# Other places in the step order for the leftover blocks' stages and expert weights

## The chip, the cores and the metric

One core of one Trainium2 chip runs the whole program. The metric is device time in microseconds (us), as the median of three executions; the profile is of one further execution.

## What is computed

Agent attention, and then a mixture of experts that sends each token to one expert. B = 4, N = 11456 tokens, C = 128, 49 agents, 8 experts of 128 → 1024 → 128:

```python
def sm(a, b):
    s = scale * (a @ b.transpose(0, 2, 1))
    s = s - s.max(-1, keepdims=True)
    e = np.exp(s)
    return e / (e.sum(-1, keepdims=True) + 1e-09)
agent_v = sm(agents, k) @ v
x = (sm(q, agents) @ agent_v).reshape(B * N, C)
logits = x @ w_gate
expert_idx = np.argmax(logits, axis=1)
gate_w = softmax(logits)[np.arange(B * N), expert_idx]
for e in range(8):                       # out starts as zeros
    mask = expert_idx == e
    h = np.maximum(x[mask] @ w1[e], 0.0)
    out[mask] = gate_w[mask, None] * (h @ w2[e])
```

## The kernel before

**Main work.** For each batch one main expert is run densely on all tokens (`experts`), in 23 groups of four tiles of 128 tokens (the last of two of 96) times 8 slices of the hidden layer: 184 steps. A step is two matmuls into `ph` (L1198, L1199), a relu on ScalarE (L1204), the low half of the f16 pair `hh` on VectorE (L1205), and five steps later twelve matmuls into `py` (L1218). Two buffers of `ph` lie between TensorE and the other two, so a step's L1198 waits for an earlier step's L1205. Every eighth step a group is stored (L1231, and a DMA on SP, L1294). While a batch is in its experts, the attention of the next, or here of the batch's own last chunks, goes between the steps: transposes through SP (`hT` L387 and L391, `M` L630), matmuls on them (L415, L639), and the routing's small VectorE work.

**Leftover blocks.** Tokens whose expert isn't the batch's main one are run in blocks of 128. Twelve blocks, of batches 0 to 2, are prepared during the experts of the last batch in three groups of four (the first, second and third group here); two more, of all batches, make the late group. `prepare_blocks` prepares a group in stages:

- slot flags `fo` (L961), then rank indices `fri` (L971) and an indirect gather of `fg` on the POOL queue, one for each block (L222);
- the `fr` chain on VectorE (L983 to L1005), which reads `fg`, yields token indices `ftr` (L997), and gathers `fx` with them (L222);
- a ScalarE copy of `fx` (L1011), TensorE transposes of it (L1017), the copy `fae` (L1018), and small loads on SP (L1016);
- two matmul stages (L1023, L1032) that end in the block's scaled input `xs` (L1040, L1041).

Ahead of the second and the third of these stands a `hold`: the next relu of the main work takes a column of the hold's tile as its bias (then it stands as L1202), and the stage behind it needs that tile's buffer. So the stage can't be ordered ahead of that step, but earlier steps can run late and it may still wait for the gather.

**Weights.** `weights_ahead(u)` requests the two f32 matrices of block u's expert on SP (`w1e` L241, `w2e` L243). `weights_split(u, j)` makes an f16 pair of one of them, on ScalarE (L1057) and VectorE (L1059). Seven blocks' weights are requested and split in the last batch, the other seven in the loop behind it, where all blocks are computed.

**What sets the order.** Everything is pushed on a heap with a time in steps and emitted in the order of these times; the order is also the priority for the scheduler that fixes each engine's order of instructions, and it may bring ready work forward. The last batch begins at `l0`. A group begins at `l0 + FG + FGI * g`, its stages at the offsets of `FST` from there (`FLS` for the late group at `l0 + FL + 2`). Weights are requested at `l0 + FW + FWJ * u` and split `FS` steps later. SP, VectorE, ScalarE and TensorE each run their instructions in order, so one that waits holds those behind it. Steps are counted below from the first L1198 of the last batch.

Of the kernel before, what the change touches and what calls it, by code (L numbers as in the profile page):

```python
# [60 lines left out]


NSE, NSL, UG = 12, 2, 4
FE, FG, FGI, FST = 34, 38, 32, (0, 4, 11, 12.5, 21, 22.5, 30, 35)
FL, FLS, FW, FWJ, WA, FS, SPA, FSE = 152, (0, 2, 9, 10.5, 18, 19.5, 26, 29), 104, 10.5, 7, 8, 7, 'D'
TSE, BL = 'D', 2
AHEAD = 3

# [1298 lines left out]
```

## Time and profile before

| | |
|---|---|
| median of three executions | 1198.95 us (1197.06 to 1199.13) |
| profiled execution | 1206.96 us |
| its span, first to last instruction | 1205.3 us |
| mean granted TensorE clock | 0.943 of full speed |
| TensorE busy | 1046.4 us, 87% |
| VectorE busy | 1050.3 us, 87% |
| ScalarE busy | 853.1 us, 71% |

The profiled execution is 8.0 us longer than the median. Busy shares are means over the whole span; the experts of the last batch, in which all changed work lies, are the stretch from about 895 to 1146 us.

### The profile page before, as it was taken

To read this page: it belongs to the slowest core of one execution; us is meant where nothing else is said; L and a number is where in the kernel's file an instruction comes from. 1 tells how busy PE (TensorE), PEld (TensorE's weight loads), DVE (VectorE), ACT (ScalarE), POOL (GpSimd) and SP (SyncE) were. 2 spreads that over 40 slices of the span, in tenths; PEclk is the share of its full clock that TensorE was granted. 3 is DMA by queue.
4 is the path that set the end of the run, shared out by engine and by line. 5 is a ranking of instruction groups with operands and counts; after the bars stand their busy time and mean duration, and the time that the engine had idled before them with its cause. 6 is when DMAs were issued, how large, how long until landed. Compare 5 with 4: busy or idle time off the path is not lost. (4 is left out here: it accounts for less than half of the span.)

```text
span 1205.3 us, 36167 instructions
## 1 busy us (share of the span) xinstructions
PE 1046.4 (87%) x14654; PEld 839.7 (70%) x14654; DVE 1050.3 (87%) x2733; ACT 853.1 (71%) x1530; POOL 179.2 (15%) x234
## 2 busy tenths in 40 slices
PE   6666899988898899998987899999989898989895
PEld 5563677766777677777766677777767676767685
DVE  7768899989788899999978899999899888989685
ACT  8737788769658688779667797787575555756481
POOL 0120000015300000123300000225100112110123
PEclk9656999989898999999999999999999999999998
DMA  8449999552279799662399799450564545423370
GB/s 319 127 99 257 258 207 218 159 158 75 52 213 251 164 206 217 190 150 89 81 245 253 156 230 209 131 145 31 141 171 115 120 98 105 141 67 109 120 249 15
DMA packets 265675, 191.05 MB, mean 159 GB/s; under 512 B 217513, under 2 KB 230306, under 8 KB 265504
## 3 DMA queue, kind: packets, MB, share of 16 engines
q1 hardware_dynamic: 263936, 186.44, 61.0%
q0 software_dynamic: 1568, 2.25, 1.0%
q8 instruction: 116, 1.90, 0.6%
q14 instruction: 55, 0.45, 0.1%
HBM read 99.75 MB, written 36.43 MB: 113 GB/s over the span
## 5 line engine op out<-in xcount | busy, mean ns | idle before, releaser
L1218 PEld LDWEIGHTS <-hh 128*128 128x128 f16 x8640 | 557.1, 100 | 171.2 <-issue 12.8
L1218 PE MATMUL py<-w2h,hh 128*128 128x128 f16 (+1 forms) x5760 | 617.2, 222 | 3.4 <-issue 1.7
L1204 ACT ACTIVATE hh<-ph 128x512 f16<-128x512 f32 (+1 forms) x728 | 410.3, 584 | 195.6 <-PE ph L1199 181.7
L1218 PE MATMUL py<-w2l,hh 128*128 128x128 f16 (+1 forms) x2880 | 532.8, 222 | 0.5 <-issue 0.5
L1205 DVE SCALAR_TENSOR_TENSOR hh<-ph,hh 128x512 f16<-128x512 f32 (+1 forms) x736 | 479.2, 667 | 37.4 <-ACT hh L1204 33.6
L1198 PE MATMUL ph<-M,Ah 128*128 128x512 f16 (+1 forms) x736 | 280.1, 381 | 36.4 <-DVE hh L1205 30.3
L1199 PE MATMUL ph<-M,Al 128*128 128x512 f16 (+1 forms) x736 | 280.0, 381 | 0.0
L362 DVE SCALAR_TENSOR_TENSOR hl<-ld,mul,hl 128x1024 f16<-128x1024 f32 (+1 forms) x126 | 155.7, 1239 | 11.6 <-ACT hl L360 10.8
L360 ACT ACTIVATE hl<-ld,mul 128x1024 f16<-128x1024 f32 (+1 forms) x126 | 136.1, 1089 | 30.6 <-DVE mul L214 30.3
L328 ACT ACTIVATE jk<-ld 128x1024 f16<-128x1024 f32 (+1 forms) x138 | 139.0, 1007 | 25.7 <-DMA ld<-in_q_dram 18.8
L1199 PEld LDWEIGHTS <-Al 128*128 128x128 f16 x736 | 72.8, 99 | 41.4 <-issue 39.4
L415 PEld LDWEIGHTS <-hT 128*128 128x128 f16 (+1 forms) x630 | 53.4, 99 | 36.3 <-DMA hT<-hl 35.2
L624 POOL TENSOR_TENSOR mm<-E,mm 128x392 f16<-128x392 f32 (+1 forms) x18 | 19.8, 1103 | 393.6 <-DVE mm L620 348.7
L1198 PEld LDWEIGHTS <-Ah 128*128 128x128 f16 x736 | 74.1, 101 | 5.2 <-issue 2.5
L415 PE MATMUL ps_s<-agh,hT 128*128 128x49 f16 x572 | 54.5, 187 | 22.6 <-DMA hT<-hl 20.5
L1231 DVE TENSOR_TENSOR yo<-py,cs 128x512 f32<-128x512 f32 (+1 forms) x92 | 61.4, 667 | 0.3 <-PE py L1218 0.3
L416 PE MATMUL ps_s<-agl,hT 128*128 128x49 f16 x572 | 54.0, 186 | 0.6 <-issue 0.6
L417 PE MATMUL ps_s<-agh,hT 128*128 128x49 f16 x572 | 53.9, 186 | 0.5 <-issue 0.5
L416 PEld LDWEIGHTS <-hT 128*128 128x128 f16 (+1 forms) x630 | 52.7, 99 | 1.8 <-issue 1.4
L493 POOL TENSOR_TENSOR es<-es,S 128x392 f32<-128x392 f32 (+1 forms) x39 | 38.5, 988 | 99.2 <-ACT S L483 75.6
L417 PEld LDWEIGHTS <-hT 128*128 128x128 f16 (+1 forms) x630 | 52.7, 99 | 0.6 <-issue 0.3
L613 ACT ACTIVATE E<-E,ln,div 128x392 f32<-128x392 f32 (+1 forms) x48 | 33.2, 691 | 20.1 <-DVE E L608 20.0
(307 smaller groups left out, 1530.7 us busy)
## 6 DMA issues: line engine op xcount, KB each, us to landing
ld<-in_k_dram SPq DMA_DIRECT2D x44, 512.0 KB
ld<-in_v_dram SPq DMA_DIRECT2D x44, 512.0 KB
ld<-in_q_dram SPq DMA_DIRECT2D x44, 512.0 KB
out_dram<-yo SPq DMA_DIRECT2D x88, 256.0 KB
w1e<-in_moe_w_dram SPq DMA_DIRECT2D x18, 512.0 KB
w2e<-in_moe_w_dram SPq DMA_DIRECT2D x18, 512.0 KB
exps<-E SPq DMA_DIRECT2D x44, 196.0 KB
wn<-in_moe_w_dram SPq DMA_DIRECT2D x16, 512.0 KB
```

What stands on the lines that cost most here:

```text
L328: nc.scalar.activation(jk[:p, :t * D], x[:p, :t, :].rearrange("p t d -> p (t d)"), AF.Square, accum_out=ss[:p])
L360: nc.scalar.activation(hi[:p, :t, :], x[:p, :t, :], AF.Copy, scale=m)
L362: nc.vector.scalar_tensor_tensor(lo[:p, :t, :], x[:p, :t, :], m, hi[:p, :t, :], op0=ALU.mult, op1=ALU.subtract)
L415: nc.tensor.matmul(o, x[:, 0, i, :p], AG["h"], start=True, stop=False)
L416: nc.tensor.matmul(o, x[:, 0, i, :p], AG["l"], start=False, stop=False)
L417: nc.tensor.matmul(o, x[:, 1, i, :p], AG["h"], start=False, stop=True)
L1198: nc.tensor.matmul(ph[:, :nn], st['Ah'][:, f, :], m, start=True, stop=False)
L1199: nc.tensor.matmul(ph[:, :nn], st['Al'][:, f, :], m, start=False, stop=True)
L1204: nc.scalar.activation(hh[:, 0, :nn], ph[:, :nn], AF.Relu)
L1205: nc.vector.scalar_tensor_tensor(hh[:, 1, :nn], ph[:, :nn], 0.0, hh[:, 0, :nn], op0=ALU.max, op1=ALU.subtract)
L1218: mm_ = lambda l, r, **k: nc.tensor.matmul(o, l, r, skip_group_check=True, **k)
L1231: nc.vector.tensor_tensor(yo[:p, :n, :], py[:p, :n * D].rearrange("p (i d) -> p i d", d=D), cs.unsqueeze(2).broadcast_to([p, n, D]), op=AL ...
```

## The change

Only times in the step order change. The first group's table is built 4 steps earlier, the three groups begin at steps 34, 62 and 90 instead of 38, 70 and 102. The `fr` chain is planned 13.5 steps behind the request of its gather instead of 8.5, and the copy of `fx` 16 steps behind the `fr` chain instead of 10; the later stages move along. In the late group the distances become 11.5 and 12 instead of 8.5 and 9. Weights are requested from step 92 on instead of 104, and split 14 steps later instead of 8, so the first split is planned at 106 instead of 112.

```diff
 NSE, NSL, UG = 12, 2, 4
-FE, FG, FGI, FST = 34, 38, 32, (0, 4, 11, 12.5, 21, 22.5, 30, 35)
-FL, FLS, FW, FWJ, WA, FS, SPA, FSE = 152, (0, 2, 9, 10.5, 18, 19.5, 26, 29), 104, 10.5, 7, 8, 7, 'D'
+FE, FG, FGI, FST = 30, 34, 28, (0, 4, 16, 17.5, 32, 33.5, 40, 45)
+FL, FLS, FW, FWJ, WA, FS, SPA, FSE = 152, (0, 2, 12, 13.5, 24, 25.5, 30, 33), 92, 10.5, 7, 14, 7, 'D'
```

On VectorE, the late group's index chain L983, which reads the gather `fg`, and the steps' L1205 ahead of it. Before:

```order
L1205 SCALAR_TENSOR_TENSOR hh<-ph,hh 128x512
L1059 SCALAR_TENSOR_TENSOR wsp<-w1e,tsm_18812,wsp 128x1024
L1205 SCALAR_TENSOR_TENSOR hh<-ph,hh 128x512 x2
L1059 SCALAR_TENSOR_TENSOR wsp<-w2e,tsm_18816,wsp 128x1024
L1205 SCALAR_TENSOR_TENSOR hh<-ph,hh 128x512 x2
L983 TENSOR_TENSOR fr_22368<-tsl,fg 128x2
L1205 SCALAR_TENSOR_TENSOR hh<-ph,hh 128x512
L984 TENSOR_TENSOR fm<-fg,fr_22368 128x180
```

Now, from the index L971 that the gather is requested with:

```order
L971 TENSOR_TENSOR fri<-frf,trb 128x2
L1205 SCALAR_TENSOR_TENSOR hh<-ph,hh 128x512
L993 TENSOR_SCALAR fr_22448<-fpc 128x2
L1059 SCALAR_TENSOR_TENSOR wsp<-w1e,tsm_18738,wsp 128x1024
L1205 SCALAR_TENSOR_TENSOR hh<-ph,hh 128x512 x3
L1059 SCALAR_TENSOR_TENSOR wsp<-w2e,tsm_18742,wsp 128x1024
L1205 SCALAR_TENSOR_TENSOR hh<-ph,hh 128x512 x2
L1059 SCALAR_TENSOR_TENSOR wsp<-w1e,tsm_18738,wsp 128x1024
L1205 SCALAR_TENSOR_TENSOR hh<-ph,hh 128x512 x3
L1231 TENSOR_TENSOR yo<-py,cs 128x512
L1205 SCALAR_TENSOR_TENSOR hh<-ph,hh 128x512
L1059 SCALAR_TENSOR_TENSOR wsp<-w2e,tsm_18742,wsp 128x1024
```

Behind the last of these rows follow one L1205 and then L983. From L971 to L983 there are now eleven steps; before there were seven.

On TensorE, the late group's transposes L1017, which read the ScalarE copy of `fx`. Before:

```order
L1198 LDWEIGHTS Ah
L1198 MATMUL ph<-M,Ah 128x512
L1199 LDWEIGHTS Al
L1199 MATMUL ph<-M,Al 128x512
L1017 MATMUL ps_small<-ident,fx_22590 49x128 x2
L1218 LDWEIGHTS hh
L1218 MATMUL py<-w2h,hh 128x128
```

Now, where ScalarE makes the copy behind the relu of step 179:

```order
L1218 LDWEIGHTS hh
L1218 MATMUL py<-w2h,hh 128x128
L1017 MATMUL ps_small<-ident,fx_22705 49x128 x2
L1198 LDWEIGHTS Ah
L1198 MATMUL ph<-M,Ah 128x192
L1199 LDWEIGHTS Al
L1199 MATMUL ph<-M,Al 128x192
```

L1017 went from step 174 to the end of step 179. The copy went from step 173 to step 179, and L997 of the same group from 168 to 171.

On SP, the requests around the last `exps` store of the last batch (96x98), which follows ScalarE's step 102. Before:

```order
L1294 DMA exps<-E 96x98
L630 DMA_TRANSPOSE M<-mm_140 128x2x96
L241 ISA
L241 DMA w1e<-in_moe_w_dram 128x1024
L243 ISA
L243 DMA w2e<-in_moe_w_dram 128x1024
L1294 DMA out_dram<-yo 128x512
```

Now:

```order
L1294 DMA exps<-E 96x98
L241 ISA
L241 DMA w1e<-in_moe_w_dram 128x1024
L243 ISA
L243 DMA w2e<-in_moe_w_dram 128x1024
L630 DMA_TRANSPOSE M<-mm_140 128x2x96
L241 ISA
L241 DMA w1e<-in_moe_w_dram 128x1024
L243 ISA
L243 DMA w2e<-in_moe_w_dram 128x1024
L241 ISA
L241 DMA w1e<-in_moe_w_dram 128x1024
```

The pairs of blocks 1, 2 and 3 now stand behind one another on SP, with one small transpose between; before, stores and the loads of L1016 lay between them. ScalarE splits them at steps 105 to 113.

## Rows read from the trace of the kernel before

**Rows 1.** The page: span, and busy time of each engine.

```profile
span 1205.3 us, 36167 instructions
PE 1046.4 (87%) x14654; PEld 839.7 (70%) x14654; DVE 1050.3 (87%) x2733; ACT 853.1 (71%) x1530; POOL 179.2 (15%) x234
```

**Rows 2.** Windows: from:to us, length, busy of PE, PEld, DVE, ACT, POOL, PEclk, DMA share, GB/s.

```profile
1060.00:1080.00 20.00, 15.20 (x168) 11.39 (x166) 16.95 (x48) 8.04 (x15) 4.02 (x4) 0.91 0.20 59
1120.00:1140.00 20.00, 14.61 (x160) 10.88 (x159) 13.68 (x34) 8.41 (x16) 2.29 (x2) 0.93 0.38 114
```

**Rows 3.** Waits of PE, 1040 to 1064: us in total, times, longest.

```profile
PE ph L1198 <- DVE hh L1205: 3.2, 2, 2.3
```

**Rows 4.** Timeline of PE and DVE, third group: start, us, instruction, [idle before, releaser].

```profile
1055.89 0.38 PE L1198 MATMUL ph<-M,Ah 128*128 128x512 f16 x1
1056.99 0.38 PE L1198 MATMUL ph<-M,Ah 128*128 128x512 f16 x1
...
1058.39 0.17 DVE L983 TENSOR_TENSOR fr<-tsl,fg 128x4 f32<-128x4 f32 x1 [1.51 <-DMA fg<-ranks,fri]
...
1062.80 0.68 DVE L1205 SCALAR_TENSOR_TENSOR hh<-ph,hh 128x512 f16<-128x512 f32 x1
1063.54 0.38 PE L1198 MATMUL ph<-M,Ah 128*128 128x512 f16 x1 [2.28 <-DVE hh L1205]
```

**Rows 5.** Timeline of ACT and PE, third group: the copy of fx, and its transposes.

```profile
1071.24 0.36 ACT L1011 COPY fx<-fx 128x196 f32<-128x196 f32 x1 [0.33 <-DMA fx<-exps,ftr]
1071.65 0.53 PE L1017 MATMUL ps_small<-ident,fx 128*49 128x128 f32 x3 [2.50 <-ACT fx L1011]
```

**Rows 6.** Windows of PE alone: busy, PEclk, DMA share, GB/s.

```profile
1072.00:1074.00 2.00, 2.00 (x18) 0.61 0.00 0
1074.00:1076.00 2.00, 2.00 (x17) 0.53 0.84 221
...
1138.00:1140.00 2.00, 2.00 (x16) 0.50 0.62 227
```

**Rows 7.** Timeline of ACT, DVE and PE, late group.

```profile
1124.80 1.15 ACT L1057 ACTIVATE wsp<-w1e,tsm 128x1024 f16<-128x1024 f32 x1 [3.64 <-DMA w1e<-in_moe_w_dram]
1125.47 0.16 DVE L983 TENSOR_TENSOR fr<-tsl,fg 128x2 f32<-128x2 f32 x1 [2.47 <-DMA fg<-ranks,fri]
1127.21 0.38 PE L1198 MATMUL ph<-M,Ah 128*128 128x512 f16 x1 [1.76 <-DVE hh L1205]
1136.94 0.27 ACT L1011 COPY fx<-fx 128x98 f32<-128x98 f32 x1 [3.05 <-DMA fx<-exps,ftr]
1137.27 0.65 PE L1017 MATMUL ps_small<-ident,fx 128*49 128x128 f32 x2 [3.00 <-ACT fx L1011]
```

**Rows 8.** Timeline of DVE, first group.

```profile
963.75 0.17 DVE L983 TENSOR_TENSOR fr<-tsl,fg 128x4 f32<-128x4 f32 x1 [0.68 <-DMA fg<-ranks,fri]
```

**Rows 9.** Timeline of POOL: the last gather request of fg, third and late group.

```profile
1052.40 1.01 POOL L222 DMA_INDIRECT fg<-ranks,fri  x1 [0.30 <-issue]
1116.14 1.01 POOL L222 DMA_INDIRECT fg<-ranks,fri  x1 [0.30 <-DMA w1e<-in_moe_w_dram]
```

**Rows 10.** Timeline of ACT: the exponent L613 ahead of the last exps store, and a split.

```profile
1039.19 0.46 ACT L613 ACTIVATE E<-E,ln,div 96x98 f32<-96x98 f32 x1
1053.47 1.14 ACT L1057 ACTIVATE wsp<-w2e,tsm 128x1024 f16<-128x1024 f32 x1
```

**Rows 11.** Windows, all engines, columns as in rows 2.

```profile
1040.00:1060.00 20.00, 18.04 (x228) 13.83 (x226) 17.23 (x42) 15.82 (x27) 4.03 (x4) 1.00 0.47 150
1113.00:1125.00 12.00, 12.00 (x156) 9.40 (x153) 9.11 (x22) 6.51 (x11) 2.02 (x2) 1.00 0.65 215
1146.00:1166.00 20.00, 19.80 (x331) 19.59 (x330) 17.82 (x32) 18.01 (x32) 4.67 (x3) 1.00 0.89 291
```

**Rows 12.** Timeline of PE, first group's stretch: matmuls that wait for SP's transposes.

```profile
955.96 0.20 PE L415 MATMUL ps_s<-agh,hT 128*128 128x49 f16 x1 [1.47 <-DMA hT<-hl]
960.17 0.38 PE L639 MATMUL ps_s<-Gs,M 128*128 128x18 f16 x8 [2.34 <-DMA M<-mm]
```

## The prediction

> **What bounds the kernel now.** I read the page first: TensorE and VectorE are both busy 87% of the span [rows 1], so neither bounds it alone, and the 13% has to be looked for by place. Then windows of 20 us over the last batch, where all the moved work lies. In two of them TensorE falls far behind: 15.20 of 20 us busy from 1060 on, and 14.61 from 1120 on, with a granted clock of 0.91 and 0.93 [rows 2]. These are where the third and the late group are prepared. Third, the waits and the timeline in those stretches, to see what ends last. The undisturbed pace is one step in 1.10 us (two successive L1198 at 1055.89 and 1056.99) [rows 4].
>
> In the third group VectorE's L983 waits 1.51 us for the gather `fg`; it stands ahead of the steps' L1205, and TensorE's L1198 waits behind these, 2.28 us at 1063.54 [rows 4], 3.2 us in two waits over that stretch [rows 3]. Then L1017 holds TensorE for 2.50 us. Its releaser, ScalarE's copy, had itself waited only 0.33 us for the gather [rows 5]: so only that part is the DMA's, and the other 2.17 us come from L1017 standing one step behind the copy in program order. After it TensorE runs at a clock of 0.61 and 0.53 for 4 us [rows 6], which costs (0.39 + 0.47) x 2 = 1.7 us.
>
> In the late group three things wait at once: ScalarE's weight split 3.64 us for `w1e`, VectorE's L983 2.47 us for `fg`, and TensorE 1.76 us behind both [rows 7]. These overlap and are not added: TensorE's 1.76 us is what is lost. Then the copy of `fx` waits 3.05 us for its gather, L1017 3.00 us behind it, all of it the DMA's [rows 7], and behind the gap the granted clock is 0.50 [rows 6], the lower of its two levels (1.2 of 2.4 GHz), which I price as the fall above, 1.7 us.
>
> **What the change gives.** Third group: L971 to L983 goes from seven steps (107 to 114) to twelve (95 to 107), five steps or 5.5 us more for a wait of 1.51: it goes. Of the other 1.7 us of L1198's wait, which come from `fr` chain and routing work lying together between the L1205 up to 1062.80 [rows 4], I take back 1.5, because the chain now comes seven steps ahead of where it was and fewer routing instructions stand with it. L1017 gives 0.33; its order (one step behind the copy, 123 and 124) is unchanged. With 2.17 us of that wait left, half the fall of the clock goes, 0.9. Sum 1.5 + 1.5 + 0.3 + 0.9 = 4.2 us. Between bounds of 1.8 (the two DMA waits alone) and 7.4 (3.2 + 2.5 + 1.7).
>
> Late group: L971 to L983 goes from seven steps to eleven, 4.4 us against 2.47: TensorE's 1.8 us go. L997 to the copy goes from five steps to eight, 3.3 us against 3.05, so the gather is just in time; but L1017 now stands at the end of step 179, right behind that step's relu and copy on ScalarE, so I leave 0.7 us there and take 2.3. The fall of the clock goes with the gap, 1.7. Sum 5.8; bounds 4.1 and 6.5.
>
> First group: the wait of 0.68 us [rows 8] goes, and VectorE has some slack there: 0.5. The second group has no wait of this kind to give. **Gains 10.5 us.**
>
> **What the change costs.** *Weights in a burst.* Three pairs now stand behind the last `exps` store on SP. That store follows ScalarE's L613 at 1039.19, and the split at the same place in the order ended its wait for data by 1053.47 [rows 10]: 14.3 us. Six matrices of 128 x 1024 f32 and two stores of 128 x 512 are 3.15 + 0.52 = 3.67 MB. At the 291 GB/s of the stretch from 1146 on this takes 12.6 us; at the 215 of the stretch from 1113 on, where weights and a gather met, 17.1 us, or 2.8 late; at the 150 of the stretch from 1040 on, 24.5 us, or 10.2 late [rows 11]. Such lateness reaches TensorE less 1.9 us, as 3.64 on ScalarE came out as 1.76 [rows 7]. I take 215 GB/s, because that stretch is nearest in kind: 2.8 - 1.9 = 0.9 us. Bounds 0 and 2.6 (with a clock fall), and the case of 150 is a rival.
>
> By the Trainium skill, "DMA: Bandwidth & Descriptors", section "Specifications", one core's HBM limit is some 358 GB/s; an estimate from that page makes the burst 10.3 us, and the term 0. No run here shows that rate held over such a stretch.
>
> *A crowd at steps 79 to 103.* The second group's chain now falls on the attention of chunk 10. The VectorE split that `hT`'s transposes need stands at step 79 and TensorE's L415 at 84, five steps where there were six; `M` and L639 likewise (84 and 89). VectorE, SP and TensorE's order are all in this path. Where such waits happen now they are 1.47 and 2.34 us [rows 12]. A step less each is 2 x 1.1 = 2.2 us, which I take; bounds 0 and 1.47 + 2.34 + 1.7 = 5.5.
>
> *The first group's L1017* is one step behind its copy, not two as before: between 0 and the 2.17 us of the third group; as ScalarE has less to do there, 0.7.
>
> Requests, hold memsets and gathers keep their number; SP's earlier requests are hidden, since SP has nothing behind them for some steps except the small transposes counted above. **Losses 3.8 us.**
>
> On the gathers first the rows: from the last request of `fg` to L983 passed 1058.39 - 1052.40 = 6.0 us in the third group, and 1125.47 - 1116.14 = 9.3 us in the late one, with weights in flight [rows 4, 7, 9]. The Trainium skill, same page, section "Issuing engines are not separate DMA queues", says that DMAs issued from any engine share the same 16 DMA engines and interleave, which speaks against more weights in flight beside a gather; the trace agrees with its 3.3 us more. By it, the third group's `fx` gather, which now starts at the end of the burst, would come 3.3 us later. With the twelve steps that it has (13.2 us) the sum stays as it is.
>
> **Sum.** 10.5 - 3.8 = 6.7 us off the profiled 1206.96, so 1200.3; that execution lies 8.0 us above the median of 1198.95, and I carry the difference over: **1192.3 us**.
>
> **Rivals.**
> - *The burst decides (slower).* At 150 GB/s ScalarE's splits come 10.2 us late, and the relus of all steps stand behind them. TensorE loses 10.2 - 1.9 + 1.7 = 10.0. Then 10.5 - 2.9 - 10.0 = -2.4: 1201.4. It decides from about 166 GB/s down (7.8 us late). For it: 150 is what that stretch moves now; against: a stretch moves only what is asked of it, and 291 was reached.
> - *The waits only move.* Crowd 5.5, L1017 2.2 and burst 0.9 make 8.6. Against gains of 10.5 down to the direct ones of 5.9 (1.5 + 0.3 + 1.8 + 2.3), that gives 1197.0 to 1201.7, in the middle 1199.3, no change. For it: VectorE is as busy as TensorE, so the chain has no free place; against: the two bad windows are far worse than the rest.
> - *Everything is kept.* All waits above go and no cost shows: 3.2 + 2.5 + 1.7 + 1.8 + 3.0 + 1.7 + 0.7 = 14.6, or 1184.4.
> - *The weights are not ahead.* The order shows the pair of block 1 requested behind step 102 and split from 105 on, three steps, not 14. If the late pair gains nothing either, the 1.8 us stays: 1194.1.
>
> **How the numbers follow.** 0.2%, or 2.4 us, is about what a measurement of this kernel can tell from no change. Forecast 0.42, with its own range of 1188 to 1196.5; everything kept 0.10; weights not ahead 0.06; waits only move 0.22; burst 0.12; a crowd beyond its bound 0.08. Faster: most of the first three, and a little of the fourth, 0.60. Same: most of the fourth and a few hundredths of the others, 0.19. Slower: most of the last two and a rest of the fourth, 0.21. The range runs from near everything kept to beyond the burst's price, 1185.5 to 1202.5, and leaves out some 2 in 10: gains beyond, a slower burst, or the direct gains alone with all losses.
>
> **What would show it.** Right: L983's waits for `fg` gone in three groups, L1017's two waits down from 5.5 us to 2 or 3, a granted clock of 1.00 where it was 0.93 in the late group's window, TensorE over 18 of 20 us there. Wrong: ScalarE waiting for `w1e` or `w2e` at the splits of steps 105 to 113, with TensorE idle behind it; new waits at L415, L639 or L1023 around step 84 to 103 with a fall of the clock; or L1198 waiting longer for L1205 where the chains now lie. What would make the whole wrong is a TensorE gap long enough for another clock fall in a stretch that is full now.

## The result, and the profile after

The changed kernel takes 1179.7 us (median of four, 1176.43 to 1183.45) against 1198.49 us before on the same chip: a ratio of 0.9846, 95% interval 0.9807 to 0.9884. Measured once more beside other kernels it gave 0.9899 (0.9856 to 0.9942). It is faster, as forecast, but by 18.8 us in the first measurement and by some 11 to 12 in the second, where 6.2 to 6.7 had been forecast. 1179.7 lies below the range of 1185.5 to 1202.5; the second ratio, on 1198.49, would be 1186.4, just inside it. Executions more than 1.5% above the fastest of their kernel (1230 to 5669 us) are left out of all ratios here and below, and one of them was the profiled execution of the run in which only the late group doesn't wait, so no trace of that run is read.

The page of the changed kernel, its span and busy times, answers to [rows 1]:

```profile
span 1175.2 us, 36166 instructions
PE 1033.2 (88%) x14654; PEld 830.2 (71%) x14654; DVE 1047.5 (89%) x2733; ACT 854.2 (73%) x1530; POOL 179.3 (15%) x234
```

The two profiled executions lie 30.1 us apart, much more than the medians. To see where, I take the starts of the store multiplications L1231 on VectorE as milestones; there are 92 in all, and the last batch's are numbers 70 to 92. Rows of the timeline, before:

```profile
911.68 0.68 DVE L1231 TENSOR_TENSOR yo<-py,cs 128x512 f32<-128x512 f32 x1
...
1029.67 0.68 DVE L1231 TENSOR_TENSOR yo<-py,cs 128x512 f32<-128x512 f32 x1
...
1114.47 0.68 DVE L1231 TENSOR_TENSOR yo<-py,cs 128x512 f32<-128x512 f32 x1
...
1150.36 0.42 DVE L1231 TENSOR_TENSOR yo<-py,cs 96x256 f32<-96x256 f32 x1 [0.34 <-PE py L1218]
```

And of the changed kernel:

```profile
899.91 0.68 DVE L1231 TENSOR_TENSOR yo<-py,cs 128x512 f32<-128x512 f32 x1
...
1011.23 0.68 DVE L1231 TENSOR_TENSOR yo<-py,cs 128x512 f32<-128x512 f32 x1
...
1089.21 0.68 DVE L1231 TENSOR_TENSOR yo<-py,cs 128x512 f32<-128x512 f32 x1
...
1118.11 0.41 DVE L1231 TENSOR_TENSOR yo<-py,cs 96x256 f32<-96x256 f32 x1
```

These are stores 70, 80, 88 and 92 of each. Up to store 70 the changed kernel is 11.8 us ahead; no instruction of VectorE stands in another place up to there, so this is the two executions' own difference (the one of before lay 8.0 us above its median, the one after 2.8 below). From store 70 to 80 it gains 118.0 - 111.3 = 6.7 us, from 80 to 88 84.8 - 78.0 = 6.8, from 88 to 92 35.9 - 28.9 = 7.0. From there to the end it loses 57.1 - 54.9 = 2.2. The sum is the 30.1.

A second profile was taken of each of the two kernels, among the runs below. Stores 80, 88 and 92 of before:

```profile
1019.32 0.68 DVE L1231 TENSOR_TENSOR yo<-py,cs 128x512 f32<-128x512 f32 x1
...
1101.56 0.68 DVE L1231 TENSOR_TENSOR yo<-py,cs 128x512 f32<-128x512 f32 x1
...
1136.69 0.42 DVE L1231 TENSOR_TENSOR yo<-py,cs 96x256 f32<-96x256 f32 x1 [0.33 <-PE py L1218]
```

And of the changed kernel:

```profile
1020.18 0.68 DVE L1231 TENSOR_TENSOR yo<-py,cs 128x512 f32<-128x512 f32 x1
...
1098.11 0.68 DVE L1231 TENSOR_TENSOR yo<-py,cs 128x512 f32<-128x512 f32 x1
...
1127.01 0.41 DVE L1231 TENSOR_TENSOR yo<-py,cs 96x256 f32<-96x256 f32 x1
```

From store 80 to 88 these give 82.2 us before and 77.9 after, from 88 to 92 35.1 and 28.9.

The windows in which the third and late group stand now (columns as in [rows 2]):

```profile
1020.00:1040.00 20.00, 17.87 (x217) 13.96 (x218) 18.51 (x50) 17.27 (x35) 1.08 (x2) 1.00 0.58 194
1040.00:1060.00 20.00, 19.65 (x240) 15.25 (x238) 19.91 (x50) 12.60 (x29) 2.94 (x3) 1.00 0.42 136
1060.00:1080.00 20.00, 18.86 (x238) 14.73 (x236) 19.89 (x58) 12.96 (x24) 0.00 (x0) 1.00 0.20 68
1100.00:1120.00 20.00, 19.77 (x280) 17.42 (x279) 14.84 (x45) 10.97 (x28) 2.01 (x2) 1.00 0.33 101
```

In none of them is TensorE below 17.8 of 20 us, where it had 15.20 and 14.61, and the granted clock is 1.00 (the upper of the two levels, 2.4 GHz) in all four. The instructions of [rows 4, 5, 7] in the timeline of the changed kernel:

```profile
1030.18 0.16 DVE L983 TENSOR_TENSOR fr<-tsl,fg 128x4 f32<-128x4 f32 x1
...
1047.57 0.36 ACT L1011 COPY fx<-fx 128x196 f32<-128x196 f32 x1
...
1047.98 0.64 PE L1017 MATMUL ps_small<-ident,fx 128*49 128x128 f32 x4
...
1101.89 0.16 DVE L983 TENSOR_TENSOR fr<-tsl,fg 128x2 f32<-128x2 f32 x1
...
1111.96 0.27 ACT L1011 COPY fx<-fx 128x98 f32<-128x98 f32 x1
...
1112.29 0.42 PE L1017 MATMUL ps_small<-ident,fx 128*49 128x128 f32 x2
```

None has a bracket (the idle time before an instruction): nothing waits for a gather any more. What waits in its place, on ScalarE and TensorE from 925 to 1115 us (us in total, times, longest):

```profile
ACT jk L328 <- DMA ld<-in_q_dram: 5.2, 1, 5.2
ACT wsp L1057 <- DMA w1e<-in_moe_w_dram: 1.2, 2, 0.6
...
PE ph L1198 <- DVE hh L1205: 8.8, 9, 3.5
PE ps_small L855 <- DVE cp L847: 1.1, 1, 1.1
PE ps_s L639 <- DVE hb L210: 0.5, 1, 0.5
PE ps_s L639 <- DVE frf L970: 0.5, 1, 0.5
PE ps_s L639 <- DMA M<-mm: 0.3, 1, 0.3
PE ps_small L1017 <- ACT fx L1011: 0.2, 1, 0.2
```

L1017's 5.5 us (3.9 in the second profile of before) are down to 0.2; the burst of weights makes ScalarE wait 1.2 us in two pieces, and behind them TensorE waits 0.2 us. The crowd that I feared shows as 1.3 us at L639, and nothing at L415. New is the wait for a load of q. The timeline of the changed kernel there:

```profile
934.56 0.34 SPq L1294 DMA_DIRECT2D out_dram<-yo  x1
935.52 0.34 SPq L284 DMA_DIRECT2D ld<-in_q_dram  x1
...
941.37 1.06 ACT L328 ACTIVATE jk<-ld 128x1024 f16<-128x1024 f32 x1 [5.16 <-DMA ld<-in_q_dram]
...
943.04 1.89 DVE L1205 SCALAR_TENSOR_TENSOR hh<-ph,hh 128x512 f16<-128x512 f32 x3 [4.36 <-ACT hh L1204]
943.78 0.59 PE L1198 MATMUL ph<-M,Ah 128*128 128x512 f16 x1 [3.54 <-DVE hh L1205]
```

SP requests the load only behind a store, ScalarE wants it before it has landed, and the relus behind it wait, and TensorE 3.54 us behind them.

### The profile page after: what moved, and what is told of

Its sections match the earlier page's. It is cut to its first block, busy times and chain, and to the rows that moved or that the text cites. A ratio compares the mean times of both kernels' runs of the same rounds, so it can differ in the third digit from the quotient of the medians.

```text
span 1175.2 us, 36166 instructions
## 1 busy us (share of the span) xinstructions
PE 1033.2 (88%) x14654; PEld 830.2 (71%) x14654; DVE 1047.5 (89%) x2733; ACT 854.2 (73%) x1530; POOL 179.3 (15%) x234
## 5 line engine op out<-in xcount | busy, mean ns | idle before, releaser
L1218 PEld LDWEIGHTS <-hh 128*128 128x128 f16 x8640 | 549.1, 99 | 164.5 <-issue 5.3
L1218 PE MATMUL py<-w2h,hh 128*128 128x128 f16 (+1 forms) x5760 | 608.3, 220 | 0.6 <-DVE Ld L643 0.4
L1218 PE MATMUL py<-w2l,hh 128*128 128x128 f16 (+1 forms) x2880 | 526.0, 220 | 0.0
L1205 DVE SCALAR_TENSOR_TENSOR hh<-ph,hh 128x512 f16<-128x512 f32 (+1 forms) x736 | 480.1, 669 | 26.6 <-ACT hh L1204 23.7
L328 ACT ACTIVATE jk<-ld 128x1024 f16<-128x1024 f32 (+1 forms) x138 | 139.2, 1009 | 30.2 <-DMA ld<-in_q_dram 24.0
L415 PEld LDWEIGHTS <-hT 128*128 128x128 f16 (+1 forms) x630 | 53.9, 99 | 32.4 <-DMA hT<-hl 31.8
L415 PE MATMUL ps_s<-agh,hT 128*128 128x49 f16 x572 | 54.9, 187 | 19.0 <-DMA hT<-hl 17.6
L1231 DVE TENSOR_TENSOR yo<-py,cs 128x512 f32<-128x512 f32 (+1 forms) x92 | 61.6, 670 | 0.0
L613 ACT ACTIVATE E<-E,ln,div 128x392 f32<-128x392 f32 (+1 forms) x48 | 33.3, 693 | 18.5 <-DVE E L608 18.4
```

Of the source, the lines that this page charges most:

```text
L328: nc.scalar.activation(jk[:p, :t * D], x[:p, :t, :].rearrange("p t d -> p (t d)"), AF.Square, accum_out=ss[:p])
L415: nc.tensor.matmul(o, x[:, 0, i, :p], AG["h"], start=True, stop=False)
L1205: nc.vector.scalar_tensor_tensor(hh[:, 1, :nn], ph[:, :nn], 0.0, hh[:, 0, :nn], op0=ALU.max, op1=ALU.subtract)
L1218: mm_ = lambda l, r, **k: nc.tensor.matmul(o, l, r, skip_group_check=True, **k)
L1231: nc.vector.tensor_tensor(yo[:p, :n, :], py[:p, :n * D].rearrange("p (i d) -> p i d", d=D), cs.unsqueeze(2).broadcast_to([p, n, D]), op=AL ...
```

## The experiments

All ratios are to the kernel before on the same chip, with 95% intervals. Gains in us are worked out from the ratio; the quotient of the two medians lies up to some 0.2% from it. My theory at the start was the sum on record: the gain is the named waits, the rest costs. The first rival: the early groups' places are worth much more than those waits. The second: the waits, with all that follows from them, are worth more than the sum says.

**The three parts alone.** The first takes only the early groups' numbers:

```diff
-FE, FG, FGI, FST = 34, 38, 32, (0, 4, 11, 12.5, 21, 22.5, 30, 35)
+FE, FG, FGI, FST = 30, 34, 28, (0, 4, 16, 17.5, 32, 33.5, 40, 45)
```

> The early groups' part alone (FE, FG, FGI, FST as in the changed kernel; late group and weights as before). My account of the waits gives it 4.2 + 0.5 - 2.2 - 0.7 = 1.8 us off the median before (1198.5), so about 1196.5. The rival, that the early groups' stages cost much more than the named waits (knock-on stalls and clock falls between 965 and 1060 us as well), gives 9 us or more, 1189 or below.

Measured: 0.9927 (0.9903 to 0.9951), 8.7 us of 1193.95. The second takes only the weights:

```diff
-... 104, 10.5, 7, 8, 7, 'D'
+... 92, 10.5, 7, 14, 7, 'D'
```

> The weights' part alone (FW 92, FS 14). My account: the burst costs 0.9, and the late stall of 1.8 may ease, so 1197 to 1200. The rival that earlier requests are worth as much as the groups: 4 us or more, 1194.5 or below. A third, that the burst costs: 1201 or above.

Measured: 0.9939 (0.9914 to 0.9963), 7.3 us less, where the sum had a loss of 0.9. The third takes only the late group's offsets:

```diff
-FL, FLS = 152, (0, 2, 9, 10.5, 18, 19.5, 26, 29)
+FL, FLS = 152, (0, 2, 12, 13.5, 24, 25.5, 30, 33)
```

> The late group's part alone (FLS with 11.5 and 12 steps of distance). My account: 1.8 + 2.3 + 1.7 = 5.8 us less, about 1192.7. If ScalarE's wait of 3.64 us for its weights stays and holds TensorE alone, only 4.0: 1194.5. The rival, that the late group's waits only move to step 179: 1198 to 1199.

Measured: 0.9971 (0.9950 to 0.9993), 3.5 us where 5.8 was expected. So, taken alone, the two parts that the sum held for nearly nothing and for a loss bring the most. But the trace of the weights' part alone shows a gather behind it. Its timeline at the late group:

```profile
1087.42 0.35 SPq L241 DMA_DIRECT2D w1e<-in_moe_w_dram  x1
...
1096.61 2.00 POOL L222 DMA_INDIRECT fg<-ranks,fri  x1 [43.47 <-DVE fr L993]
1098.91 1.01 POOL L222 DMA_INDIRECT fg<-ranks,fri  x1 [0.30 <-DMA fae<-avd]
...
1104.38 0.15 DVE L983 TENSOR_TENSOR fr<-tsl,fg 128x2 f32<-128x2 f32 x1
```

The pair of weights is requested 9.2 us ahead of the gather, not beside it, and L983 reads `fg` 5.5 us after its last request without a wait. In [rows 7, 9] the same gather took 9.3 us, and ScalarE waited 3.64 us for a `w1e`. There two pairs were requested beside it, and one beside the last gather of the third group. SP's rows of before, the first matrix of each pair, the third group's first:

```profile
1052.10 0.36 SPq L241 DMA_DIRECT2D w1e<-in_moe_w_dram  x1
...
1113.18 0.36 SPq L241 DMA_DIRECT2D w1e<-in_moe_w_dram  x1
...
1116.15 0.00 SPq L241 DMA_DIRECT2D w1e<-in_moe_w_dram  x1
```

For some runs the profile also has the time from a gather's request to its landing. For the late group's two gathers of `fg` (the median), first in the run with only the late group's offsets, whose weights are requested where they were, then in the run with only the weights' part:

```profile
fg<-ranks,fri POOLq DMA_INDIRECT x2, 8.9
...
fg<-ranks,fri POOLq DMA_INDIRECT x2, 3.6
```

The gathers of `fx`, beside which no weights are requested, took 3.9 and 3.5 us in the same two runs.

**No wait for any gather.** Before's order, in which the chain and the copy read constants; the gathers still run. Of the edit, without the lines of the chain that index `g`:

```diff
-        g = cut(g)
+        g = iota[:, :NT].unsqueeze(1).broadcast_to([P, n, NT])
 ...
-        nc.vector.tensor_tensor(ti, tr, r[5], op=ALU.add)
+        nc.vector.scalar_tensor_tensor(ti, iota[:, u0:u0 + n], float(P), pidx.broadcast_to([P, n]), op0=ALU.mult, op1=ALU.add)
 ...
-        nc.scalar.copy(cut(ex2), cut(ex))
+        nc.scalar.copy(cut(ex2), iota[:, :A].unsqueeze(1).broadcast_to([P, n, A]))
```

> The order of before with nothing waiting for a gather: the chain reads a constant in place of fg, the copy one in place of fx, the scatter goes to fixed rows; the gathers still run. So the leftover blocks' tokens are not the reference's. If the gathers' waits are the whole of the change's gain, with all that follows from them (the clock too), this is as fast as the changed kernel or faster: 1180 or below. By my own sum of the waits (1.5 + 0.3 + 0.9 + 1.8 + 3.0 + 1.7 + 0.5 = 9.7) it comes to 1189. If most of the gain comes from where the stages stand, and not from the gathers, 1192 or above.

Measured: 0.9887 (0.9865 to 0.9909), a median of 1180.96 us, by the ratio 13.5 us less than before on that chip. That is above my sum of the waits (9.7) and near the changed kernel. VectorE and ScalarE run the same instructions in the same order as before from the last batch on, but for L998, which no longer belongs to the chain. The gathers also fetch other rows and the scatter writes other rows; behind store 92, where the scatter lies, this kernel's two profiles take 56.1 and 56.2 us against 54.9 and 55.3, so nothing is gained there. The same edit on the changed kernel:

> The changed kernel's order with nothing waiting for a gather, in the way of the run on the order of before: constants in place of fg and fx, scatter to fixed rows, so the leftover blocks' tokens are not the reference's. If the change took away all that the gathers cost, this is the changed kernel's time, a ratio of 0.984 to 0.986 to before. If gathers still hold something up in the changed order, it is below: 0.980 or less.

Measured: 0.9896 (0.9851 to 0.9940), outside both expectations, which were built on the first ratio of 0.9846. Beside the changed kernel's second ratio of 0.9899, taken on another chip, taking away the gathers' waits gives nothing more: the change has left none to take. The changed kernel and before's order without waits once more, on one chip:

> The changed kernel once more, beside the other three on one chip. The theory that its whole gain is the gathers' waits expects it level with the run without those waits, within 0.3%; the rival, that its placement gives something beside them, expects it faster by 0.4% or more. Against before: a ratio of 0.984 to 0.988.

Measured: 0.9899 (0.9856 to 0.9942), less of a gain than the 0.984 to 0.988 expected.

> Before's order with nothing waiting for a gather, once more (constants in place of fg and fx, scatter to fixed rows; the leftover blocks' tokens are not the reference's). A ratio of 0.987 to 0.990 if the first measurement holds, and by the theory within 0.3% of the changed kernel on the same chip.

Measured: 0.9894 (0.9858 to 0.9930). The two ratios are 0.05% apart, as the theory of the gathers expects, but each is known only to some 0.4%; the rival, that placement gives something besides, isn't borne out here, and less than that could not be seen.

**What of the weights' part does it.** FW 92 alone, with FS left at 8:

> Before with the weights requested 12 steps earlier (FW 92) and FS left at 8. The requests on SP stand as with both numbers changed; the splits hardly move. If the earlier requests are what the weights' part gains by, because they are out of the way when the late and third group gather, the ratio is that of the weights' part, 0.992 to 0.996. If the distance between request and split is, about 1.000.

Measured: 0.9920 (0.9884 to 0.9957). In its trace the late L983 doesn't wait for `fg`, the late copy waits 1.10 us for `fx`, and from store 88 to 92 it takes 30.1 us. FS 14 alone:

> Before with FS 14 alone. The requests on SP stand where they were, and only the last four splits on VectorE move to later steps (162, 170, 181, 183). If earlier requests are the cause, this gives 1.000 (within 0.3%); if the distance, 0.992 to 0.996.

Measured: 0.9961 (0.9925 to 0.9998), whose interval nearly reaches 1. In its trace ScalarE doesn't wait for `w1e` in the late group any more, but L983 still waits 2.79 us for `fg` and the copy 3.07 us for `fx`, and from store 88 to 92 it takes 35.4 us, as before. So ScalarE's 3.64 us for `w1e` were not what held the late group. The earlier requests carry the effect; whether the later splits add a little elsewhere stays open. Then the weights' part on top of the order without waits:

> Before's order with nothing waiting for a gather, and the weights' part (FW 92, FS 14) on top; the leftover blocks' tokens are not the reference's. If earlier requests gain only by clearing the way for the gathers, this is level with the run without it, 0.988 to 0.991. If they gain by themselves (0.992 to 0.994 alone), both add up: 0.982 to 0.984.

Measured: 0.9916 (0.9884 to 0.9949), no better than without it (0.9887, 0.9894). Where nothing waits for a gather, earlier requests gain nothing. The reverse, the change without its weights' part:

> The changed kernel without the weights' part (FW 104, FS 8). If the weights gain only where a gather waits, the other two parts have taken most of that away and this is close to the changed kernel, 0.987 to 0.991. If they gain by themselves, their 0.6% is missing: 0.993 or more.

Measured: 0.9919 (0.9892 to 0.9946), between the two expectations. It lies 0.2% above the changed kernel's second measurement, well within both intervals, and 0.7% above its first, whose interval ends below this one's. So the times don't settle whether the weights are needed once the distances are long. The trace speaks for it in the late group, where a wait is left:

```profile
1126.03 0.27 ACT L1011 COPY fx<-fx 128x98 f32<-128x98 f32 x1 [2.01 <-DMA fx<-exps,ftr]
...
1126.36 0.42 PE L1017 MATMUL ps_small<-ident,fx 128*49 128x128 f32 x2 [2.13 <-ACT fx L1011]
```

From store 88 to 92 this kernel takes 31.2 us, where both profiles of the changed kernel take 28.9 and have no such wait.

**Which group's waits.** The same constants for one group at a time, with the scatter of its blocks out of bounds so that their rows aren't written:

```diff
+        nw = early and u0 == 8; g = ... if nw else cut(g)
```

> Before's order; the third group alone doesn't wait for its gathers (constants in place of fg and fx; its four blocks' rows are not written). My term for this was 4.2 us with bounds of 1.8 and 7.4; by the traces with and without all waits it is 6 to 7: a ratio of 0.994 to 0.995. If it gives 0.997 or more, the term was right and the gain lies elsewhere.

Measured: 0.9989 (0.9962 to 1.0017). In its trace the third group's L983 and copy no longer wait, but L1017 still does:

```profile
1072.51 0.64 PE L1017 MATMUL ps_small<-ident,fx 128*49 128x128 f32 x4 [2.23 <-ACT fx L1011]
```

In the second profile of before this wait is 0.88 us, and 0.18 in both runs without any gather's wait. So in one order of instructions it runs from 0.2 to 2.5 us, with a gather's wait ahead of it or without.

> Before's order; the first and the second group don't wait for their gathers (constants; their eight blocks' rows are not written). My term was 0.5 us. By the runs so far their moves are worth nothing: 0.998 to 1.000. If the waits in these two groups carry part of the 1.1% of the run without any, 0.996 or less.

Measured: 1.0000 (0.9971 to 1.0029).

> Before's order; the late group alone doesn't wait for its gathers (constants; its two blocks' rows are not written, which may take a us or two from the end). The third group's waits gave 0.9989 and the first two's 1.000, all together 0.989; if the parts add up, the late group's give 0.990. By the traces it is the 7 us between the stores of groups 18 and 22, 0.994.

Measured: 0.9962 (0.9937 to 0.9987). The late group counts most, the first two nothing. Together they make 0.5%, less than the 1.1% without all waits. The three intervals would have to lie near their lower ends for the parts to add up, so this split isn't settled.

**Versions.** The first group back at its old place, the others 26 steps apart:

> The changed kernel with the first group where it was before (FE 34, FG 38) and the others 26 steps apart (at 64 and 90). In the changed kernel's trace ScalarE waits 5.2 us for a load of q that stands behind a store on SP at step 41, and the clock falls behind it. The load now stands behind a transpose and is wanted six steps later. If that stall costs what the trace shows, some 4 us, the ratio comes to 0.981; if it is covered by what follows, 0.985 as the changed kernel.

Measured: 0.9927 (0.9895 to 0.9959), a miss of both expectations. TensorE's 3.54 us behind the load of q are gone, but ScalarE still waits for it (7.39 us by its row), and in its trace L415 and L639 wait 1.50 and 2.56 us for transposes, as in the order of before [rows 12]. The gain isn't there: from store 70 to 80 this trace needs 116.9 us, the changed kernel's 111.3. Then only the third group, the late group and the weights moved, in a table by group (OLD and NEW are the two offsets' tuples of the change):

```diff
+FE, FG, FST = 34, (38, 70, 90), (OLD, OLD, NEW)
-        at(l0 + FG + FGI * g, group, i, min(UG, NSE - i), i, True, FST)
+        at(l0 + FG[g], group, i, min(UG, NSE - i), i, True, FST[g])
```

> The changed kernel with the first and second group at their old times and offsets; only the third group (at step 90, new offsets), the late group and the weights are moved. In the traces the second group's move costs some 4 us between the stores of groups 8 and 12 (65.6 us against 60.2 to 61.6 with the old places), and the first group's is worth nothing. By that this is 4 to 5 us faster than the changed kernel, a ratio of 0.981; if the two early groups' moves gain by their waits for gathers, 0.988 or more.

Measured: 0.9895 (0.9852 to 0.9939).

> As the run with only the third group moved, with that group four steps later (94). If the third group's place itself counts little once its distances are long, the same ratio within 0.3%; if its chain must miss the last chunk's routing, slower by 2 us or more.

Measured: 0.9903 (0.9871 to 0.9936). Both are level with the changed kernel on that chip (0.9899), not 4 to 5 us faster. The moves of the first and second group neither gain nor cost that can be seen. The traces show an exchange: with the two groups moved, TensorE waits 3.4 to 3.6 us at once behind the load of q (five traces); with them at their old places, this wait isn't there, and L415 and L639 wait 1.5 and 2.3 us or more for transposes. That leaves the third group for what the early groups' part brought alone.

**No change at all.**

> The kernel before as one of the four, for a second profile and to show what the comparison gives where nothing changes: 1.000 within 0.3%. Its profile shows whether the pauses at stores 76, 79 and 80 of the first profile, 2.5 us each beyond other runs of the same order, come again.

Measured: 1.0012 (0.9981 to 1.0043). Its profile needs 113.2 us from store 70 to 80, 82.2 to 88 and 35.1 to 92, against 118.0, 84.8 and 35.9 in the first profile. The pauses come again, smaller: stores 76, 79 and 80 come 9.8, 16.1 and 8.9 us behind the store ahead of them, against 11.7, 17.2 and 10.8 in the first profile and 9.1, 14.4 and 8.1 in the run with only the late group's offsets.

## Why the prediction was wrong

The direction was right, and so was the mechanism of the gains, the gathers' waits with the clock behind them; the weights' part was priced with the wrong sign. The size was off by a factor of nearly three in the first measurement and nearly two in the second. Point by point:

- **The failed step is the weights' term: "Bounds 0 and 2.6", a loss of 0.9.** Alone this part measured a gain of 7.3 us, so a gain was not even within its bounds. I priced the requests by when their own data would be wanted, and never by whom they get out of the way of. The rows that point to it were in the prediction: 9.3 us for the late gather, 6.0 for the third group's [rows 4, 7, 9], and I used them only to ask whether a gather of the third group would be late. They are no clean contrast, though: beside the third group's last gather a pair was requested too (L241 at 1052.10), beside the late one two. The Trainium skill, "DMA: Bandwidth & Descriptors", section "Issuing engines are not separate DMA queues", has DMAs from all issuers interleave on the same engines. The runs agree: the late gather lands after 3.6 us with the pair requested well ahead, and after 8.9 with the weights requested where they were. I weighed the rule against the change, and it speaks for it. Beside the longer distances the same waits go only once: by the traces the weights' part then adds 2.3 us in the late group (31.2 and 28.9), still a gain and no loss.
- **The other two losses did not come.** "A crowd at steps 79 to 103" (2.2) and the first group's L1017 (0.7): the waits at L415, L639 and L1017 now sum to 1.5 us over the whole last batch, where L415 and L639 alone had 1.5 and 2.3 before. What came instead had no term, TensorE's 3.54 us behind the load of q, with a granted clock of 0.50 from 944 to 948 us. The two seem to offset each other: with the first two groups left where they were the time is the same (0.9895 and 0.9899).
- **Late group, 5.8 us forecast.** From store 88 to 92 the two profiles of before have 35.9 and 35.1 us, the changed kernel's two 28.9 and 28.9: 6.6 us. Nearly the term. Its waits are gone, L1017's too, where I had left 0.7. That is in part luck: I gave it all to the late group's offsets, and these alone measured 3.5 us, while the weights' part alone took this stretch to 30.2.
- **Third group, 4.2 us forecast.** From store 80 to 88: 84.8 and 82.2 before, 78.0 and 77.9 after, 5.5 us. I left 2.17 us of L1017's wait as an affair of order, one step behind the copy. That step was misread: the order is the same after the change, and L1017's row has no bracket at 1047.98; in the order of before the wait runs from 0.2 to 2.5 us. What sets it is not shown. Alone, the group's waits on the unchanged order gave no measurable gain, which I can't explain fully; in that run's trace L1017 still waits 2.23 us.
- **The end.** I had no term for what follows the last batch, and it costs 2.0 us (54.9 and 55.3 us before, 57.1 and 57.1 after).
- **First groups, 70 to 80.** The first profile shows a gain of 6.7 us here. Executions of before's order, with or without the gathers' waits, range from 109.4 to 118.3 us in this stretch, and the changed kernel's second has 111.0, so most of that can't be put down to the change.

6.6 and 5.5 less 2.0 make 10.1 us, near the second measurement (10.6 by the medians, 12.1 by the ratio) and well short of the first (18.8). Against the 6.7 of the sum that is 3.4 more: the losses of 3.8 that did not come, 0.8 in the late group and 1.3 in the third, less 0.5 for the first group and 2.0 at the end. A part of that first ratio is probably the scatter between executions: the two intervals overlap only from 0.9856 to 0.9884. The intervals of all these runs reach 0.2 to 0.45% to either side, wider than the 0.2% that the prediction counted on. Of the rivals, "everything is kept" (1184.4, a chance of 0.10) was the nearest.

What stays open: why the waits by group make 0.5% and together 1.1%, and how much of the whole time the weights' part brings beside the longer distances. Shown, to within some 0.4%, is that all the gathers' waits taken away on the old order bring as much as the change, and that neither taking them away on the new order nor earlier weights give anything beyond that.

## What to carry to other kernels

When transfers are requested earlier, ask first which other transfer they were lying beside, and what waits for that one: here large weights out of the way of a small gather gained 7 us alone, and not by the wait for the weights themselves. Take all waits of a suspected kind away at once, on the unchanged order, with constants in place of what is waited for; it shows what a rearrangement of them can bring at most. And before taking a stall in one profile as a price, look at a second profile of the same order.

## What was unexpected of the hardware

With one order of instructions, the stretch from store 70 to 80 took 110.0 us in one execution and 118.0 in another. In the long one TensorE pauses while it waits for nothing that the profile shows. Timeline of before:

```profile
973.35 0.18 PE L416 MATMUL ps_s<-agl,hT 128*128 128x49 f16 x1 [0.56 <-issue]
...
974.77 0.27 PE L1218 MATMUL py<-w2h,hh 128*128 128x128 f16 x2 [0.81 <-issue]
...
975.80 0.35 DVE L682 TENSOR_REDUCE rk<-Ld 128x24 f32<-128x192 f32 x1 [2.52 <-ACT Ld L680]
```

And the same place in the run with only the late group's offsets changed, whose order is the same there:

```profile
964.80 0.36 ACT L680 ACTIVATE Ld<-Ld 128x192 f32<-128x192 f32 x1 [0.45 <-DVE Ld L679]
...
965.29 0.33 DVE L682 TENSOR_REDUCE rk<-Ld 128x24 f32<-128x192 f32 x1
```

Behind TensorE's pause of 0.8 us VectorE waits 2.5 us for ScalarE, and store 76 comes 2.6 us later (11.7 us behind store 75, against 9.1). That the pause makes all of this is not shown, and its cause wasn't tried.
